# Three weight loads moved ahead of five stores in one DMA queue, and a 64-row tile that multiplies its high and low halves together

## The chip, the core and the metric

The kernel runs on one core of a Trainium2 chip, as one program. Its time is device time in microseconds (us), from launch to end; the median of three runs is what counts. One more execution was profiled, and every row below is from that one. TensorE (PE) does the matmuls, VectorE (DVE), ScalarE (ACT) and GpSimd (POOL) work on tiles, SyncE (SP) does nothing but start DMAs, in order.

## What is computed

Three layers follow each other: an attention with 32 memory slots, a dense MLP, and a mixture of eight experts with two experts per token. The change touches only the experts, which cut down read:

```
def _moe2_ref(x, w_gate, w_noise, noise, w1, w2):      # x: 2304 tokens x 512
    ...                                                # noisy logits, top 2 of 8 experts, their softmax
    for e in range(E):
        for k in range(2):
            mask = top2[:, k] == e
            h = np.maximum(x[mask] @ w1[e], 0.0)       # 512 -> 1024
            out[mask] += top2_w[mask, k, None] * (h @ w2[e])   # 1024 -> 512
```

## The kernel before

**Arithmetic.** Every float32 operand of a matmul is split into a high part (rounded to the format that TensorE takes, `F32R`) and a low part, the rest. A product is the sum of three: high x high, high x low and low x high. The splits are done by ScalarE (the high part) and VectorE (the subtraction).

**Parts.** The routing packs the tokens of each expert into a table. `PARTS` lists nine pieces of work, called parts 0 to 8 here (the index `k` in the code): parts 0 and 1 are the two pieces of expert 0, parts 2 to 8 are the other seven experts, the busiest first, and have room for 640, 640, 608, 608, 608, 576 and 576 tokens (`COLS`). Each of parts 2 to 8 has five token tiles, four of 128 rows and a last one of 128, 96 or 64 rows; the 64-row tiles are those of parts 7 and 8.

**One part.** `up(k, f)` computes the hidden units f * 128 to f * 128 + 127 of all tokens, in two column groups (of 320, 304 or 288 tokens) of 12 matmuls each, in PSUM tiles named `h` (two buffers) and `x2` (four buffers, shown as `x`) in turn. ScalarE takes the high part out of PSUM (`GH`, L675), VectorE the low part (`GL`, L676). After the eight `up` steps, `down(k, j)` multiplies token tile j with `w2`: for each f the three matmuls `GH` x hi, `GH` x lo, `GL` x hi, with the token tile held in the array and 512 columns of `w2` moving, 24 matmuls in all. VectorE scales the result by the routing weight and adds what the tokens hold already (`y`, L699), and GpSimd scatters it to `out` (L702).

**What is brought in beside that.** `fetch_w2` (L571) loads the part's own `w2` in four pieces of 512 KB on SP's queue into the tiles `w2s`, and `split_w2` splits each into high and low part (ScalarE L583, VectorE L584), between the PSUM evacuations of `up`. `gather(k + 1)` brings the next part's tokens: five indirect DMAs on GpSimd into `ex` (L621), five stores on SP's queue that put them into a scratch tensor `xs_d` (L623), and four loads that read them back in another layout as `xg` (L628). `earlier(k)` gathers the present values of `out` (L637). `fetch_w1(e + 1, c)` loads the next part's `w1` into two buffers `w1s` (L556), and `split_w1` splits it (ScalarE L568, VectorE L569). `flip` turns the gathered tokens and splits them (L654, L658, L659).

**What sets the order.** The code is written in program order, and a scheduler of the framework puts the instructions of each engine into one fixed order; `tc.issue_after(x)` tells it not to place what follows before `x`. Each engine, SP too, works through its list in order: an instruction that waits holds up everything behind it on that engine. In the loop of `experts`, the code of `gather(k + 1)` stands ahead of the four calls of `fetch_w2` (L728 to L729).

Of the kernel before, what the change touches and what calls it, by code (L numbers as in the profile page):

```python
# [6 lines left out]
F32 = mybir.dt.float32  # L7
F32R = mybir.dt.float32r
# [3 lines left out]
AF = mybir.ActivationFunctionType  # L12
OP = mybir.AluOpType
# [16 lines left out]
MAIN = 512  # L30
# [13 lines left out]
def body(ctx, tc, a):  # L44
# [10 lines left out]
    def psum(tag, bufs):  # L55
        return ps.tile([128, 512], F32, name=tag, tag=tag, bufs=bufs)
# [444 lines left out]
    LATEST = [None]  # L501
# [3 lines left out]

    m2 = ExitStack()
    P2 = {}
    W1S, W2S, W1, W2, TAB, GID, XG, EX, XH, XL, GH, GL = ({} for _ in range(12))
    PARTS = [(0, 0, EARLY), (0, EARLY, CT - EARLY)] + [(e, 0, CT) for e in range(1, E)]
    WIDTH = (EARLY * 128, CAP - EARLY * 128) + COLS  # L510
    ID, START, OVER = {}, {}, {}
# [59 lines left out]
    def fetch_w2(e, c):  # L571
        W2S[e, c] = P2["b"].tile([128, 2, DM], F32, name="w2s", bufs=4)
        w = a["moe2_w2"][bass.ds(ID[e], 1)] if e else a["moe2_w2"][0:1]
        sp.dma_start(W2S[e, c], w[:, c * 256:(c + 1) * 256, :].rearrange("o (c p) f -> p (o c) f", p=128))

    def split_w2(e, c):
        if c == 0:
# [25 lines left out]
        pool.tensor_scalar(GID[k][:, :n - 1], TAB[k][:, :n - 1, 0], float(N - 1), None, op0=OP.min)  # L603
        return pool.tensor_scalar(GID[k][:h, n - 1:], TAB[k][:h, n - 1:, 0], float(N - 1), None, op0=OP.min)

    def gather(k):
        if k < 3:
            for j in range(PARTS[k][2]):
                if k == 0:
                    XG[k, j] = m1.tile([128, DM], F32, name="xa", tag="st", bufs=4)  # L610
                elif j == 0:
                    t = P2["b"].tile([128, 4 * CT, 128], F32, name="xg").rearrange("p b c -> p (b c)")
                if k:
                    XG[k, j] = t[:, j * DM:(j + 1) * DM]
                last = pool.indirect_dma_start(out=XG[k, j], out_offset=None, in_=x2_d if k else x2_d[:KNOWN, :],
                                               in_offset=bass.IndirectOffsetOnAxis(ap=GID[k][:, j:j + 1], axis=0))
            return last
        for j in range(PARTS[k][2]):
            h = height(k, j)
            t = P2["b"].tile([128, DM], F32, name="ex", bufs=CT)[:h]  # L620
            last = pool.indirect_dma_start(out=t, out_offset=None, in_=x2_d,  # L621
                                           in_offset=bass.IndirectOffsetOnAxis(ap=GID[k][:h, j:j + 1], axis=0))
            sp.dma_start(xs_d[k % 2][j * 128:j * 128 + h, :], t)  # L623
        XG[k] = P2["b"].tile([128, 4 * CT, 128], F32, name="xg")
        w = WIDTH[k] // 32
        x = xs_d[k % 2].rearrange("(b i) (q c) -> q i b c", i=32, q=4)
        for q in range(4):
            sp.dma_start(XG[k][q * 32:(q + 1) * 32, :w, :], x[q][:, :w, :])  # L628
        return last
# [32 lines left out]
    def up(k, f):  # L662
        hi, lo = W1[PARTS[k][0]]
        c = slice(f * 128, f * 128 + 128)
        GH[k, f], GL[k, f] = [P2["b"].tile([128, CAP], F32R, name=f"g{x}{f}") for x in "hl"]
        cs = cuts(k)
        for i, (r0, r1) in enumerate(zip(cs, cs[1:])):
            r, w = slice(r0, r1), r1 - r0
            p = psum("x2", 4) if (f * (len(cs) - 1) + i) % 2 else psum("h", 2)
            n = 0  # L670
            for d in range(4):
                for wt, x in ((hi, XH[k]), (hi, XL[k]), (lo, XH[k])):
                    pe.matmul(p[:, :w], wt[:, d, c], x[:, d, r], start=(n == 0), stop=(n == 11))  # L673
                    n += 1
            act.activation(GH[k, f][:, r], p[:, :w], AF.Relu)  # L675
            LATEST[0] = dve.scalar_tensor_tensor(GL[k, f][:, r], p[:, :w], 0.0, GH[k, f][:, r].bitcast(F32),  # L676
                                                 op0=OP.max, op1=OP.subtract)

    def down(k, j, inside={}):
        e = PARTS[k][0]  # L680
        P = height(k, j)
        p = psum("x2", 4)[:P]
        hi, lo = W2[e]
        r = slice(j * 128, j * 128 + P)
        n, mm = 0, None
        for f in range(8):
            for g, w in ((GH[k, f], hi), (GH[k, f], lo), (GL[k, f], hi)):
                with tc.issue_after(mm.ins) if mm else ExitStack():
                    mm = pe.matmul(p, g[:, r], w[:, f, :], start=(n == 0), stop=(n == 23))  # L689
                n += 1  # L690
                if n in inside:
                    with tc.issue_after(mm.ins):
                        mm = inside[n]()
                elif not inside:
                    mm = None
        y = P2["b"].tile([128, DM], F32, name="y", bufs=3)[:P]
        w = TAB[k][:P, j, 1:2].bitcast(F32)
        if e:
            done = dve.scalar_tensor_tensor(y, p, w, EX[k, j], op0=OP.mult, op1=OP.add)  # L699
        else:  # L700
            done = dve.tensor_scalar(y, p, w, None, op0=OP.mult)
        st = pool.indirect_dma_start(out=a["out"], out_offset=bass.IndirectOffsetOnAxis(ap=TAB[k][:P, j, 0:1], axis=0),  # L702
                                     in_=y, in_offset=None, bounds_check=N - 1, oob_is_err=False)
        for o in puts:
            tc.declare_no_dep(st.ins, o.ins, reason="distinct rows, or ordered by the row that is read back")
        puts.append(st)
        return done

    def experts(late, last):
        open_b()  # L710
        for k, (e, t0, n) in enumerate(PARTS):
            first, nxt = t0 == 0, k + 1 < len(PARTS)
            new = nxt and PARTS[k + 1][0] != e
            if k == 1:
                gather(2)
                indices(3)
            elif k and nxt:
                with tc.issue_after(puts[-1].ins):
                    g = gather(k + 1)
                with tc.issue_after(g.ins):  # L720
                    g = earlier(k)
                if k + 2 < len(PARTS):
                    with tc.issue_after(g.ins):
                        indices(k + 2)
            elif k:
                earlier(k)
            if first:
                for c in range(4):  # L728
                    fetch_w2(e, c)  # L729
            for f in range(8):  # L730
                up(k, f)
                if k == 0 and f == 2:
                    late(15, 17)
                if k == 0 and f == 4:
                    routed = last(17, 18)
                    split_w2(e, 0)
                    split_w2(e, 1)
                    table(1)
                    with tc.issue_after(gather(1).ins):
                        table(2)  # L740
                        for c in range(2):
                            W1S[1, c] = P2["b"].tile([128, FE], F32, name="w1s", bufs=2)
                            pool.memset(W1S[1, c][:, :1], 0.0)
                            fetch_w1(1, c)
                        for i in range(3, len(PARTS)):
                            table(i)
                if first and f % 2 and (k or f > 3):
                    split_w2(e, f // 2)
            if nxt:
                flips = iter(range(PARTS[k + 1][2]))  # L750
                ahead = PARTS[k + 1][2] - n
                for j in range(max(1, (ahead + 2) // 2) if k else 0):
                    with tc.issue_after(LATEST[0].ins):
                        flip(k + 1, next(flips))
            if new and k > 1:
                for c in range(2):
                    fetch_w1(e + 1, c)
            for j in range(n):
                done = down(k, j, {} if k or j < n - 1 else {10: lambda: flip(1, 0), 18: lambda: flip(1, 1)})
                if nxt and k:  # L760
                    for i in range(max(1, (ahead + 2) // 2)):
                        i = next(flips, None)
                        if i is not None:
                            with tc.issue_after(done.ins) if k > 1 else ExitStack():
                                flip(k + 1, i)
                if new and j < 4:
                    split_w1(e + 1, j)
                    if j < 2:
                        fetch_w1(e + 1, j + 2)
            if new:  # L770
                for c in range(n, 4):
                    split_w1(e + 1, c)
                    if c < 2:
                        fetch_w1(e + 1, c + 2)
# [63 lines left out]
    first = ST.pop(("i", 0))  # L838
# [199 lines left out]
```

## Time and profile before

| | us |
|---|---|
| median of three runs | 869.5 (869.11, 869.5, 877.16) |
| the profiled execution's own time | 870.56 |
| its span, first to last instruction | 868.3 |
| outside the span | 2.26 |
| TensorE busy with matmuls | 821.9, 95% of the span |
| VectorE busy | 495.3, 57% |
| ScalarE busy | 362.4, 42% |
| GpSimd busy | 207.1, 24% |

The expert parts run from about 411 us to the end. In the profile PE is the matmuls and PEld the loading of the held operand, which overlaps them; `x<-w,gh` reads "tile x is written from tiles w and gh"; SPq is SP's DMA issues. A matmul's listed duration includes its way through the array, so for dense stretches the distance between starts is the better measure. PEclk is the TensorE clock that was granted, as a share of 2.4 GHz.

### The profile page before, as it was taken

What the parts mean: (1) busy time and instruction counts of PE and PEld (TensorE: products, weight loads), DVE (VectorE), ACT (ScalarE), POOL (GpSimd) and SP (SyncE); (2) the same over time, 40 slices, a digit from 0 to 9 for tenths busy, and PEclk for the clock granted to TensorE, in tenths of its full rate; (3) what the DMA queues carried; (4) which work ended last, traced back from release to release, by engine and by line L of the source; (5) the groups of instructions that cost most, each with busy time, mean ns of one, the idle gap of its engine ahead of it and who ended that gap; (6) DMA issues with size and microseconds to landing.
All of it is one profiled execution on the core that took longest, in us unless ns stands there. A gap on an engine that the chain in (4) does not pass through costs nothing. (4 is left out here: it accounts for less than half of the span.)

```text
span 868.3 us, 14165 instructions
## 1 busy us (share of the span) xinstructions
PE 821.9 (95%) x5276; PEld 697.9 (80%) x5276; DVE 495.3 (57%) x1161; ACT 362.4 (42%) x840; POOL 207.1 (24%) x237
## 2 busy tenths in 40 slices
PE   4598899999999999999999899999999999999994
PEld 2276667778887888887989888989889898897983
DVE  3898895875358747655724355354553546444510
ACT  3688886444434454552413343323333233332400
POOL 0243341022000500500452303215132151321301
PEclk9998999999999999999999899999999999999998
DMA  8897952274055215322463966765847657475200
GB/s 303 272 315 270 319 182 91 59 220 126 2 185 193 50 49 147 73 63 49 110 165 112 259 178 216 184 231 177 205 154 195 233 175 208 142 182 192 59 26 29
DMA packets 86254, 138.89 MB, mean 160 GB/s; under 512 B 13853, under 2 KB 48157, under 8 KB 86176
## 3 DMA queue, kind: packets, MB, share of 16 engines
q1 hardware_dynamic: 74976, 105.48, 40.8%
q0 software_dynamic: 11200, 32.43, 12.1%
q8 instruction: 43, 0.70, 0.4%
q14 instruction: 35, 0.29, 0.1%
HBM read 107.20 MB, written 31.26 MB: 159 GB/s over the span
## 5 line engine op out<-in xcount | busy, mean ns | idle before, releaser
L689 PE MATMUL x<-w,gh 128*128 128x512 f32 (+2 forms) x640 | 198.1, 390 | 0.0
L689 PEld LDWEIGHTS x<-w,gh 128*128 128x128 f32 (+2 forms) x640 | 116.6, 183 | 27.3
L689 PE MATMUL x<-w,gl 128*128 128x512 f32 (+2 forms) x320 | 124.7, 390 | 0.0
L673 PE MATMUL h<-xh,w 128*128 128x304 f32 (+4 forms) x512 | 120.4, 307 | 3.2 <-DVE gl L676 3.2
L673 PE MATMUL x<-xh,w 128*128 128x304 f32 (+4 forms) x512 | 119.0, 305 | 0.0
L280 PE MATMUL h<-ah,wph 128*128 128x320 f32 (+1 forms) x512 | 111.0, 304 | 4.8 <-DVE th L285 2.5
L280 PEld LDWEIGHTS h<-ah,wph 128*128 128x128 f32 x512 | 90.7, 193 | 20.8 <-DVE th L285 5.3
L305 PE MATMUL x<-gh,woh 128*128 128x512 f32 x256 | 105.9, 414 | 0.1
L702 POOL DMA_INDIRECT out<-y,tab x40 | 41.9, 1048 | 254.6 <-DVE y L699 221.6
L305 PE MATMUL x<-gh,wol 128*128 128x512 f32 x256 | 102.4, 400 | 0.0
L305 PE MATMUL x<-gl,woh 128*128 128x512 f32 x256 | 101.8, 398 | 0.6 <-DVE gc L299 0.3
L673 PEld LDWEIGHTS h<-xh,w 128*128 128x128 f32 x512 | 88.3, 190 | 4.1 <-DVE gl L676 3.4
L673 PEld LDWEIGHTS x<-xh,w 128*128 128x128 f32 x512 | 88.1, 190 | 0.0
L285 DVE SCALAR_TENSOR_TENSOR th<-th,h 128x256 f32<-128x256 f32 (+1 forms) x128 | 57.5, 449 | 51.9 <-ACT th L283 51.2
L489 POOL DMA_INDIRECT tab_d<-rows,slot x36 | 38.9, 1082 | 195.2 <-DVE slot L486 181.9
L283 ACT ACTIVATE th<-h 128x256 f32<-128x256 f32 (+1 forms) x128 | 52.3, 408 | 71.9 <-PE h L280 69.1
L673 PE MATMUL h<-xl,w 128*128 128x304 f32 (+4 forms) x256 | 78.4, 306 | 0.0
L673 PE MATMUL x<-xl,w 128*128 128x304 f32 (+4 forms) x256 | 78.3, 306 | 0.0
L280 PE MATMUL h<-ah,wpl 128*128 128x256 f32 (+1 forms) x256 | 76.8, 301 | 0.0
L289 ACT ACTIVATE gh<-th 128x256 fp32r<-128x256 f32 x128 | 53.3, 416 | 55.6 <-DVE th L285 55.5
L290 DVE TENSOR_TENSOR gl<-th,gh 128x256 fp32r<-128x256 f32 x120 | 54.6, 455 | 32.9 <-ACT gh L289 29.1
L699 DVE SCALAR_TENSOR_TENSOR y<-x,tab,ex 128x512 f32<-128x512 f32 (+2 forms) x35 | 26.2, 750 | 78.9 <-PE x L689 78.7
(183 smaller groups left out, 1332.3 us busy)
## 6 DMA issues: line engine op xcount, KB each, us to landing
w2s<-moe_w SPq DMA_DIRECT2D x32, 512.0 KB, 7.5
wi<-win_d SPq DMA_DIRECT2D x24, 512.0 KB, 7.1
w1s<-moe_w SPq DMA_DIRECT2D x24, 512.0 KB, 8.5
kv<-kv SPq DMA_DIRECT2D x16, 650.0 KB, 8.9
st<-moe_w_in SPq DMA_DIRECT2D x16, 512.0 KB, 5.2
st<-moe_w_out SPq DMA_DIRECT2D x16, 512.0 KB, 5.9
xs_d<-ex SPq DMA_DIRECT2D x25, 256.0 KB, 3.5
q<-qt SPq DMA_DIRECT2D x16, 288.0 KB, 5.4
```

The lines of the kernel that those rows point to most:

```text
L280: pe.matmul(p[:, :w], wt[:, g, c:c + 128], AH[b, g][at][:, t0:t0 + w], start=(n == 0), stop=(n == 5))
L283: act.activation(th[:, :w], p[:, :w], AF.Tanh, scale=0.5)
L285: dve.scalar_tensor_tensor(u[:, :w], th[:, :w], 1.0, p[:, :w], op0=OP.add, op1=OP.mult)
L289: act.activation(gh, u[:, :256], AF.Copy)
L290: last = (pool if b == 0 and (2 * f + i) % 4 == 0 else dve).tensor_sub(gl, u[:, :256], gh.bitcast(F32))
L305: pe.matmul(X2[key], held, moved, start=(f == 0 and n == 0), stop=(f == NF - 1 and n == 2))
L489: st = pool.indirect_dma_start(out=tab_d, out_offset=bass.IndirectOffsetOnAxis(ap=slot[:, j, k:k + 1], axis=0), in_=rows.bitcast(I32)[:, j ...
L673: pe.matmul(p[:, :w], wt[:, d, c], x[:, d, r], start=(n == 0), stop=(n == 11))
L689: mm = pe.matmul(p, g[:, r], w[:, f, :], start=(n == 0), stop=(n == 23))
L699: done = dve.scalar_tensor_tensor(y, p, w, EX[k, j], op0=OP.mult, op1=OP.add)
L702: st = pool.indirect_dma_start(out=a["out"], out_offset=bass.IndirectOffsetOnAxis(ap=TAB[k][:P, j, 0:1], axis=0), in_=y, in_offset=None, b ...
```

## The change

Three things change. First, the four `fetch_w2` calls stand ahead of `gather` in the code, and the stores of `gather` are told not to be placed before the last of these loads. Second, where a part has room for 576 tokens (parts 7 and 8), the second column group of `up` is taken out of PSUM in two pieces: the tokens up to 511 as before, and the last 64 into a tile `GB` of 128 columns that holds their high part in columns 0 to 63 and their low part in columns 64 to 127. `down` of the 64-row tile holds `GB` in the array and needs two matmuls per f, with hi and with lo; rows 0 to 63 of the result are the high part's share and rows 64 to 127 the low part's, and VectorE adds them in two operations. (The product low x low, which was left out before, comes in with this.) Third, the last part starts its `down` steps with the 64-row tile.

```diff
     def fetch_w2(e, c):
...
-        sp.dma_start(W2S[e, c], w[:, c * 256:(c + 1) * 256, :].rearrange("o (c p) f -> p (o c) f", p=128))
+        return sp.dma_start(W2S[e, c], w[:, c * 256:(c + 1) * 256, :].rearrange("o (c p) f -> p (o c) f", p=128))
...
-    def gather(k):
+    def gather(k, after=None):
...
-            sp.dma_start(xs_d[k % 2][j * 128:j * 128 + h, :], t)
+            with tc.issue_after(after.ins):
+                sp.dma_start(xs_d[k % 2][j * 128:j * 128 + h, :], t)
...
-            act.activation(GH[k, f][:, r], p[:, :w], AF.Relu)
-            LATEST[0] = dve.scalar_tensor_tensor(GL[k, f][:, r], p[:, :w], 0.0, GH[k, f][:, r].bitcast(F32),
-                                                 op0=OP.max, op1=OP.subtract)
+            parts = [(p[:, :w], GH[k, f][:, r], GL[k, f][:, r])]
+            if r1 == MAIN + 64:
+
+                GB[k, f] = P2["b"].tile([128, 128], F32R, name=f"gb{f}")
+                parts = [(p[:, :MAIN - r0], GH[k, f][:, r0:MAIN], GL[k, f][:, r0:MAIN]),
+                         (p[:, MAIN - r0:w], GB[k, f][:, :64], GB[k, f][:, 64:])]
+            for p, h, l in parts:
+                act.activation(h, p, AF.Relu)
+                LATEST[0] = dve.scalar_tensor_tensor(l, p, 0.0, h.bitcast(F32), op0=OP.max, op1=OP.subtract)
...
     def down(k, j, inside={}):
...
-        p = psum("x2", 4)[:P]
+        both = P == 64
+        p = psum("x2", 4)[:128 if both else P]
...
         for f in range(8):
-            for g, w in ((GH[k, f], hi), (GH[k, f], lo), (GL[k, f], hi)):
+            h, l, b = GH[k, f][:, r], GL[k, f][:, r], GB.get((k, f))
+            for g, w in ((b, hi), (b, lo)) if both else ((h, hi), (h, lo), (l, hi)):
                 with tc.issue_after(mm.ins) if mm else ExitStack():
-                    mm = pe.matmul(p, g[:, r], w[:, f, :], start=(n == 0), stop=(n == 23))
+                    mm = pe.matmul(p, g, w[:, f, :], start=(n == 0), stop=(n == (15 if both else 23)))
...
-            done = dve.scalar_tensor_tensor(y, p, w, EX[k, j], op0=OP.mult, op1=OP.add)
+            done = dve.scalar_tensor_tensor(y, p[:P], w, EX[k, j], op0=OP.mult, op1=OP.add)
+            if both:
+                done = dve.scalar_tensor_tensor(y, p[P:], w, y, op0=OP.mult, op1=OP.add)
...
+            if first:
+                for c in range(4):
+                    loaded = fetch_w2(e, c)
...
-                    g = gather(k + 1)
+                    g = gather(k + 1, loaded)
...
-            if first:
-                for c in range(4):
-                    fetch_w2(e, c)
...
-            for j in range(n):
+
+            for j in range(n) if nxt else (n - 1, *range(n - 1)):
```

**SP's queue in part 2.** These are SP's rows in the order before: `w2s` is part 2's own `w2`, `xs_d_67` the scratch tensor for part 3's tokens, `xg` their way back, `w1s` the next part's `w1`.

```order
L574 DMA w2s<-moe_w 128x2x512
L623 DMA xs_d_67<-ex 128x512 x5
L574 ISA
L574 DMA w2s<-moe_w 128x2x512
L574 ISA
L574 DMA w2s<-moe_w 128x2x512
L628 DMA xg<-xs_d_67 32x20x128 x4
L574 ISA
L574 DMA w2s<-moe_w 128x2x512
L556 ISA
L556 DMA w1s<-moe_w 128x1024
```

The same place of SP in the changed order, from the third of the four `w2s` loads on:

```order
L574 DMA w2s<-moe_w 128x2x512
L574 ISA
L574 DMA w2s<-moe_w 128x2x512
L624 DMA xs_d_67<-ex 128x512 x5
L556 ISA
L556 DMA w1s<-moe_w 128x1024
L556 ISA
L556 DMA w1s<-moe_w 128x1024
L629 DMA xg<-xs_d_67 32x20x128 x4
```

All four `w2s` loads stand ahead of the five stores now; what stands between the stores and the read-back are two `w1s` loads of the next part. In parts 3 to 8 SP's order was and stays: `w2s` loads, `w1s` loads, stores, read-back.

**ScalarE at the end of `up` in part 2.** Before, with `gh_5847` the high part of f = 7, the rows are:

```order
L675 ACTIVATE gh_5847<-h 128x320
L675 ACTIVATE gh_5847<-x_5864 128x320
L658 ACTIVATE xh<-xt 128x4x128
L583 ACTIVATE w_5673<-w2s 128x512 x2
L568 ACTIVATE w_5927<-w1s 128x512 x4
```

And in the changed order:

```order
L683 ACTIVATE gh_5847<-h 128x320
L568 ACTIVATE w_5927<-w1s 128x512
L683 ACTIVATE gh_5847<-x_5864 128x320
L568 ACTIVATE w_5927<-w1s 128x512 x3
L659 ACTIVATE xh<-xt 128x4x128 x2
```

The last two splits of `w2s` have moved up into the middle of `up`, and a split of the next part's `w1s` now stands ahead of the last evacuation of `up`; VectorE's list has the same shift.

**TensorE in part 8.** The last tile before began with these rows, with `gh_8657` and `gl_8658` for f = 0, three matmuls for each f:

```order
L689 MATMUL x_9051<-w_8721,gh_8657 64x512
L689 MATMUL x_9051<-w_8722,gh_8657 64x512
L689 MATMUL x_9051<-w_8721,gl_8658 64x512
L689 MATMUL x_9051<-w_8721,gh_8689 64x512
L689 MATMUL x_9051<-w_8722,gh_8689 64x512
```

In the changed order the tile comes first, right behind `up`'s last matmul (L674), with two matmuls for each f, and four tiles of 128 rows follow:

```order
L674 MATMUL x_8950<-xh,w_8510 128x288
L698 MATMUL x_8972<-w_8744,gb_8704 128x512
L698 MATMUL x_8972<-w_8745,gb_8704 128x512
L698 MATMUL x_8972<-w_8744,gb_8739 128x512
L698 MATMUL x_8972<-w_8745,gb_8739 128x512
```

The row count of the whole list falls from 4306 to 4290, that is 8 matmuls less for each of parts 7 and 8.

## Rows read from the trace of the kernel before

**Rows 1.** Windows: start:end length, busy PE PEld DVE ACT POOL; PEclk, DMA share, GB/s.

```profile
489.80:493.13 3.33, 0.16 (x2) 0.00 (x0) 1.14 (x3) 1.81 (x4) 1.69 (x4) 0.87 1.03 346
493.13:499.13 6.00, 6.00 (x23) 6.00 (x23) 3.44 (x7) 2.15 (x6) 0.00 (x0) 0.51 1.14 206
...
506.46:857.19 350.73, 350.73 (x1994) 312.50 (x1992) 166.43 (x289) 109.96 (x225) 93.34 (x97) 1.00 0.56 167
857.19:868.30 11.11, 0.00 (x1) 0.00 (x0) 0.74 (x1) 0.00 (x0) 0.92 (x1) 0.67 0.03 8
```

**Rows 2.** Timeline of PE in part 2: start, duration, line, tiles [idle before].

```profile
489.65 0.31 PE L673 MATMUL x<-xh,w 128*128 128x320 f32 x1
493.13 0.64 PE L673 MATMUL h<-xh,w 128*128 128x320 f32 x1 [3.17 <-DVE gl L676]
...
499.42 0.31 PE L673 MATMUL h<-xh,w 128*128 128x320 f32 x1
...
506.46 0.63 PE L689 MATMUL x<-w,gh 128*128 128x512 f32 x2
```

**Rows 3.** Timelines of ACT (two rows) and DVE (one row) in part 2.

```profile
480.37 0.65 ACT L583 ACTIVATE w<-w2s 128x512 fp32r<-128x512 f32 x1
...
491.32 0.63 ACT L583 ACTIVATE w<-w2s 128x512 fp32r<-128x512 f32 x1 [7.93 <-DMA w2s<-moe_w]
...
492.59 0.48 DVE L676 SCALAR_TENSOR_TENSOR gl<-h,gh 128x320 fp32r<-128x320 f32 x1
```

**Rows 4.** Timeline of SP's DMA issues in part 2; xN merges N issues.

```profile
466.60 0.40 SPq L574 DMA_DIRECT2D w2s<-moe_w  x1
478.37 7.66 SPq L623 DMA_DIRECT2D xs_d<-ex  x5
486.23 0.98 SPq L574 DMA_DIRECT2D w2s<-moe_w  x2
```

**Rows 5.** Timeline of POOL: the first of five gathers for part 3.

```profile
474.23 1.50 POOL L621 DMA_INDIRECT ex<-x_d,gid  x1 [0.30 <-issue]
```

**Rows 6.** Tile w2s over the whole run, its 32 loads.

```profile
DMA to landing us min/median/max: 5.1/7.5/12.9
```

**Rows 7.** Tile w1s from 470 us on, its 24 loads.

```profile
DMA to landing us min/median/max: 3.6/8.5/9.3
```

**Rows 8.** Windows, columns as in Rows 1, just ahead of the gathers.

```profile
472.00:474.00 2.00, 2.00 (x15) 1.89 (x15) 2.00 (x4) 1.64 (x3) 1.19 (x1) 1.00 0.00 0
```

**Rows 9.** Timeline of PE in part 7: its fourth and fifth tile, then part 8.

```profile
793.27 0.62 PE L689 MATMUL x<-w,gh 128*128 128x512 f32 x2
...
798.71 0.63 PE L689 MATMUL x<-w,gh 128*64 128x512 f32 x2
...
804.23 0.29 PE L673 MATMUL h<-xh,w 128*128 128x288 f32 x1
```

**Rows 10.** Groups by form, PEld of L689: count | busy, mean ns | idle before.

```profile
L689 PEld LDWEIGHTS x<-w,gh 128*128 128x128 f32 x560 | 104.5, 188 | 21.1
...
L689 PEld LDWEIGHTS x<-w,gh 128*64 128x64 f32 x32 | 4.3, 134 | 2.9
```

**Rows 11.** Groups by form: 64-column pieces on DVE and ACT, columns as in Rows 10.

```profile
L299 DVE TENSOR_TENSOR gc<-th,gc 128x64 fp32r<-128x64 f32 x64 | 17.9, 280 | 0.0
L298 ACT ACTIVATE gc<-th 128x64 fp32r<-128x64 f32 x64 | 15.6, 243 | 0.0
```

**Rows 12.** Timeline of DVE around the 64-row tile of part 7.

```profile
800.49 0.43 DVE L659 TENSOR_TENSOR xl<-xt,xh 128x256 fp32r<-128x256 f32 x1 [0.48 <-ACT xh L658]
804.43 0.74 DVE L699 SCALAR_TENSOR_TENSOR y<-x,tab,ex 64x512 f32<-64x512 f32 x1 [3.51 <-PE x L689]
```

**Rows 13.** Windows, columns as in Rows 1: a full tile's store, then the last one.

```profile
853.00:854.00 1.00, 1.00 (x6) 0.56 (x5) 0.00 (x0) 0.00 (x0) 0.70 (x1) 1.00 0.00 0
854.00:855.00 1.00, 1.00 (x6) 0.58 (x5) 0.00 (x0) 0.00 (x0) 0.00 (x0) 1.00 0.74 262
...
859.00:860.00 1.00, 0.00 (x0) 0.00 (x0) 0.00 (x0) 0.00 (x0) 0.17 (x1) 1.00 0.25 59
```

More of the change, by code (lines that the diff above doesn't have):

```diff
@@ L507, in body @@
     P2 = {}
-    W1S, W2S, W1, W2, TAB, GID, XG, EX, XH, XL, GH, GL = ({} for _ in range(12))
+    W1S, W2S, W1, W2, TAB, GID, XG, EX, XH, XL, GH, GL, GB = ({} for _ in range(13))
     PARTS = [(0, 0, EARLY), (0, EARLY, CT - EARLY)] + [(e, 0, CT) for e in range(1, E)]
```

## The prediction

> **What bounds the kernel now.** I read the busy shares first, then PE by stages, then what ended PE's idle time, and from there the queues. TensorE is busy for 95% of the span, so only two things can shorten the expert parts: fewer matmuls, or time in which PE stands still or runs slowly. The windows show where that is [rows 1]: from 506.46 us to PE's end at 857.19 its busy time equals the length of the stretch, with the clock at 1.00; there is nothing to win there but matmuls. The one hole is in part 2, at 489.80 to 493.13, and behind it a stretch at half clock (0.51, the lower level of 1.2 GHz), which ends at about 499.1.
>
> What caused it is read backwards. PE waited for VectorE's low part `gl` [rows 2], which ran at 492.59 [rows 3]. That in turn stood in VectorE's and ScalarE's lists behind a split of `w2s`, and ScalarE had waited 7.93 us for that load [rows 3]. The load was issued at 486.23 only, directly behind five stores that kept SP from 478.37 to 486.03 [rows 4]. The stores wait for GpSimd's gathers, of which the first was issued at 474.23 [rows 5]. The first `w2s` piece, which stood ahead of the stores, went out at 466.60 and was in time. So the second piece was late because of its place in SP's list, not for want of bandwidth.
>
> **The loads in front.** Cost of the hole, start to start: 493.13 - 489.65 = 3.48 us, less one matmul's distance. That distance at full clock: from 499.42 to 506.46 PE did four groups of 12, so 7.04 / 48 = 0.147 us [rows 2]. Hole: 3.33 us. From 493.13 to 506.46 it did six groups, 72 matmuls, which need 10.56 us at 0.147 and took 13.33: 2.77 us for the half clock. Together **6.10 us**. Behind it PE is dense to its end [rows 1], so what is won here is carried through.
>
> Does it all go? With the new order the second to fourth `w2s` pieces follow the first, at about 467 to 468.1 (0.49 each, from the two in 0.98 [rows 4]). The slowest `w2s` load of the run took 12.9 us [rows 6], so 481.0 is the latest landing; the median 7.5 gives 475.6. In the new order the second piece's split stands two evacuations earlier than before, directly behind the split that ran at 480.37 [rows 3], so it is wanted from about 480.9, the others some 2 us and 3.5 us later. Even the slowest would be just in time, and there is room behind it: ScalarE's wait began at 491.32 - 7.93 = 483.39 and PE stopped 6.4 us later, at 489.80; it went on 1.8 us after the wait's end. So PE would stop for a piece that lands later than 480.9 + 6.4 - 1.8 = 485.5 only. In the new order up to three splits, 1.95 us of ScalarE at most [rows 3], come between two evacuations that PE brings 1.76 us apart (12 x 0.147); the few tenths are taken up by the two buffers of `h`.
>
> What is moved past: the stores, and behind them two `w1s` loads of part 3's expert and the read-back. The stores need the gathers, which the moved 1.5 MB could slow. The DMA engines stood empty from 472 to 474 (share 0.00 [rows 8]), with the first gather at 474.23; the moved loads fill that gap and overlap the gathers until about 476 to 478, so they could hold the stores up by 3 us at most. The Trainium skill ("DMA: Bandwidth & Descriptors", Queues, rings and completion order) says that each DMA engine takes turns, packet by packet, between the queues that have work, which speaks against the move: loads put ahead take half of the gathers' engines while they last. By that rule the first store would come later and the time would stay as it is; no row of this trace shows the overlap.
>
> The new late thing can only be `w1s`. Its first two loads leave at 486.23, in the place that the `w2s` loads had, and take 8.5 us, at most 9.3 [rows 7]: landed at 494.7 to 495.5. ScalarE wants the first one behind the evacuation of `up`'s last `h` group: `up` ends at 506.46 - 6.10 = 500.36, that group 1.76 us earlier at 498.6, its evacuation by 499.0. Slack 3.5 us, or 0.5 with the stores 3 us late. And a `w1s` that is late costs nothing on PE until PE needs f = 7 of the first `down` tile, its 22nd matmul, 21 x 0.227 = 4.8 us behind 500.36. I put this at nothing; its other end is a rival below.
>
> **The pair.** A 128-row tile takes 798.71 - 793.27 = 5.44 us for 24 matmuls, 0.227 each; the 64-row tile takes 804.23 - 798.71 = 5.52, though it holds half the columns [rows 9]: the price is the moving 512 columns. Sixteen matmuls with 128 held columns, the form of the row of 5.44, take 3.63. Won: 1.89 in part 7 and 1.89 in part 8, **3.78 us**. The lower bound is what it would be if wider weight loads were in the open. A 128-column load shows 188 ns and a 64-column one 134 [rows 10], 54 ns more; 16 x 0.054 = 0.86 us a tile, leaving 0.95 each. I take the row of 5.44, since it has the same loads in it and 188 ns is under the distance of 227. The Trainium skill ("TensorE: Matmul & The Clock Gate", LDWEIGHTS) has a load's time go with the held columns, not the rows, which is the rule against this edit: the 54 ns between the rows agree with it. By that rule in the open the two tiles would save 1.9 us in all; the distances say it is hidden.
>
> Added beside PE: in each of 16 column groups one more evacuation of 64 columns, at most 0.243 us on ScalarE and 0.280 on VectorE [rows 11], in groups that PE needs some 1.6 us for (288 of 320 columns of 1.76), on engines busy 42% and 57%; the PSUM tile is held that much longer, with four buffers. Hidden. One more `y` operation for each of the two tiles, as long as the 0.74 of the first [rows 12]: in part 7 it delays the store and the gathers of `out` behind it by that, which part 8 first uses some 25 us later; in part 8 the tile is first, so it isn't at the end. The shorter tile of part 7 lets part 8 start at 802.34 instead of 804.23; its last tokens are split at 800.92 [rows 12], 1.4 us ahead. If that were late, it would cost what it is late by.
>
> **The order of the last part.** The last store is a full tile now. A full tile's bytes moved up to 855.0 at most, 1.3 us behind the end of its issue at 853.70; the last one's were done by 860.0, 0.8 behind its issue's end at 859.17 [rows 13]. So the tail of 11.11 us [rows 1] grows by about **0.5 us**. A gain is excluded, since there are no fewer rows in any store; bounds 0 (the landing is covered by what else ends the program) and 1.0 (a whole slice of the window).
>
> **Sum.** 6.10 + 3.78 - 0.5 = 9.4 us. The profiled execution had 868.3 + 2.26 = 870.56 us, so 861.2 on its scale. It stands 1.06 above the median of 869.5. If profiling costs that throughout, the median goes to 860.1; if the other runs have a smaller hole, to 861.2. No row tells; the hole can't be much smaller in them, since the half clock alone makes 2.77 of it and the fastest run is only 1.45 below. I forecast **860.3 us**, 1.06% under 869.5.
>
> **Rivals.**
>
> *The `w1s` loads inherit the stall.* They sit behind the same stores, and ScalarE has a split of them ahead of `up`'s last evacuation. For: nothing but a row of SP's list changed. Against: 3.5 us of slack, and another 6 before PE feels it. It decides from a landing at 503.9 on (505.1 less the split and the evacuation). At 507 it costs 3.1 and about 2.8 for the clock that then falls, and the time is 866.2. It ends **slower than before** from a landing at 510.5, 24 us behind the issue, where a hole of 6.6 and 2.8 of half clock have eaten the 9.4; at 513 the time is 872. That is more than twice the slowest 9.3.
>
> *Part of the hole stays,* because the moved loads share the engines with what else is there at 467 to 478 and a piece lands at 487.5 instead of 485.5. Against: that is 19 us behind its issue, and the first one, issued there, was in time. Price: 2 us of hole and a clock that stays up or falls, 862.3 to 865.1.
>
> *The pair doesn't pay:* the wider loads come out, or the 64-row tile's new waits stall PE. 862.2 to 864.1. Against: rows 9.
>
> *The change doesn't do what it says,* the hole being made elsewhere and only shown there. 3.3 us from the pair alone, 866.2. Against: the chain from the store to the hole has no link without a row.
>
> **How the numbers follow.** The forecast gets 0.76, the pair that doesn't pay 0.08, the inherited stall with a gain left 0.05 and slower than before 0.03, a hole that stays in part 0.05, the last 0.03. The forecast's own spread: upward 0.5 for the tail's bound and up to 1.45 for a smaller hole, downward 0.5 for the tail and 0.4, by which the fastest run lies under the median; so 859.4 to 862.3. The range of 858.6 to 863.6 takes in the nearer parts of the rivals. About 1% is what a measurement of this kernel can tell from no change: 860.8. It lies within the forecast's spread, with some 0.7 of it below: 0.53 faster, and the rest with the rivals that keep a gain or none, 0.44; 0.03 slower.
>
> **What would show it.** Right: SP's four `w2s` issues together at 466 to 468 us; no wait of ScalarE for `w2s` in part 2; PE dense from 472 to its end with the clock at 1.00; `up` of part 2 ending at about 500.4; the tiles of 64 rows at 3.6 us each; PE's end at about 847.3; a tail of 11.6. Wrong: a wait of PE at about 505, a distance above 0.227 in the 64-row tiles, or idle time ahead of part 8's first matmul.

## The result, and the profile after

The changed kernel takes **862.69 us** (median of five runs, 860.93 to 865.03). The kernel before, run beside it, took 872.91 us (869.11 to 877.16). The ratio of the runs is 0.9891, with a 95% interval of 0.9861 to 0.9920 (that of the two medians is 0.9883): **1.1% faster**. The forecast was 860.3 with a range of 858.6 to 863.6, 1.06% under the 869.5 known then.

I compare the two traces by one stretch, from the first `up` matmul of part 2 to the end of TensorE's last matmul. It holds all of the change but the tail, and what happens ahead of part 2 can't blur it. Before it took 857.19 - 471.85 = 385.34 us. After it takes 850.85 - 475.39 = 375.46. The difference is **9.88 us; the two terms of the sum gave 6.10 + 3.78 = 9.88.** (That it agrees to the hundredth owes something to luck: both terms were read from this same profile of before, and against its second profile, further down, the difference is 7.66.)

First SP's DMA issues in part 2 of the kernel after (start, duration, line, tiles), against [rows 4]:

```profile
470.10 2.62 SPq L574 DMA_DIRECT2D w2s<-moe_w  x4
482.09 8.34 SPq L624 DMA_DIRECT2D xs_d<-ex  x5
490.69 0.96 SPq L556 DMA_DIRECT2D w1s<-moe_w  x2
492.79 3.24 SPq L629 DMA_DIRECT2D xg<-xs_d  x4
```

All four `w2s` loads leave together, 5.29 us ahead of the stretch (before, the first did so 5.25 us ahead). The first store follows the first gather (477.76) by 4.33 us, where it was 4.14 in [rows 4, 5]. Next ScalarE's splits in the same part, against [rows 3]; a bracket would be idle time and what ended it:

```profile
483.07 0.64 ACT L583 ACTIVATE w<-w2s 128x512 fp32r<-128x512 f32 x1
483.90 1.69 ACT L583 ACTIVATE w<-w2s 128x512 fp32r<-128x512 f32 x3
485.78 1.18 ACT L583 ACTIVATE w<-w2s 128x512 fp32r<-128x512 f32 x2
487.14 1.19 ACT L583 ACTIVATE w<-w2s 128x512 fp32r<-128x512 f32 x2
...
503.95 0.63 ACT L568 ACTIVATE w<-w1s 128x512 fp32r<-128x512 f32 x1 [1.17 <-PE x L674]
```

The wait of 7.93 us is gone, and the first `w1s` split, where the stall might have gone, waits for a matmul and not for a load. What PE makes of it, by windows (start:end length, busy time of PE, PEld, DVE, ACT, POOL; granted clock, DMA share, GB/s), against [rows 1]:

```profile
475.39:503.89 28.50, 28.50 (x195) 28.25 (x194) 14.72 (x28) 11.74 (x26) 12.17 (x13) 1.00 0.91 258
503.89:850.85 346.96, 346.95 (x1978) 312.12 (x1976) 168.46 (x305) 111.16 (x239) 92.98 (x97) 1.00 0.57 169
850.85:861.80 10.95, 0.00 (x0) 0.00 (x0) 0.75 (x1) 0.00 (x0) 0.97 (x1) 0.69 0.08 28
```

`up` of part 2 takes 28.50 us with PE full throughout, and PE stays full at clock 1.00 to its end. The tail of 11.11 has become 10.95. The 64-row tile of part 7 and the first matmul of part 8, in PE's timeline, against [rows 9]:

```profile
796.15 3.80 PE L698 MATMUL x<-w,gb 128*128 128x512 f32 x16
799.78 0.29 PE L674 MATMUL h<-xh,w 128*128 128x288 f32 x1
```

From start to start it is 3.63 us, where it was 5.52: won 1.89 in part 7.

The stretch began 3.54 us later than before, though up to part 2's `w2s` loads every engine's list is the same. The two profiled executions differ, piece by piece, as follows: 870.56 - 9.88 (stretch) + 3.54 (ahead of it) - 0.16 (tail) - 0.50 (outside the span: 1.76, before 2.26) = 863.56. The 0.50 comes with the programs: the time outside the span is 2.12 to 2.27 us in all runs of before that have it, 1.73 to 1.80 in those of after, and no run shows why. The 3.54 is a balance. Until 353 us after was 2.62 us ahead of before, most of it won from 68 to 77 us, where the granted clock was 0.62 in before and 1.00 in after. Two holes then cost it some 6 us, with the half clock behind the first; "issue" means that the profile shows nothing that PE waited for:

```profile
356.49 0.62 PE L280 MATMUL h<-ah,wph 128*128 128x256 f32 x2 [2.59 <-issue]
...
457.45 0.28 PE L674 MATMUL h<-xl,w 128*128 128x256 f32 x1 [1.02 <-issue]
```

### The profile page after: what moved, and what is told of

Its sections match the earlier page's. It is cut to its first block, busy times and chain, and to the rows that moved or that the text cites. A ratio compares the mean times of both kernels' runs of the same rounds, so it can differ in the third digit from the quotient of the medians.

```text
span 861.8 us, 14168 instructions
## 1 busy us (share of the span) xinstructions
PE 813.7 (94%) x5260; PEld 693.9 (81%) x5260; DVE 497.9 (58%) x1179; ACT 364.1 (42%) x856; POOL 206.9 (24%) x237
## 4 chain that ended last, share of the span: by engine, by line
PE 80%; DVE 8%; ACT 4%; DMA 3%; issue 2%; POOL 1%; SPq 1%; POOLq 0%; ACTq 0%
PE x L698 25%; PE x L305 18%; PE x L674 12%; PE h L674 12%; PE h L280 9%; PE aux L149 2%; DMA st<-moe_w_out 1%; DMA kv<-kv 1%; DVE gl L290 1%; PE aux L127 1%; DVE th L285 1%; POOL wo L224 1%; ACT lw L203 1%; DVE wo L209 1%; ACT th L283 1%
## 5 line engine op out<-in xcount | busy, mean ns | idle before, releaser
L698 PE MATMUL x<-w,gh 128*128 128x512 f32 (+1 forms) x608 | 188.0, 390 | 0.0
L698 PEld LDWEIGHTS x<-w,gh 128*128 128x128 f32 (+1 forms) x608 | 112.4, 186 | 24.4
L674 PE MATMUL h<-xh,w 128*128 128x304 f32 (+4 forms) x512 | 119.1, 304 | 0.3 <-issue 0.3
L698 PE MATMUL x<-w,gl 128*128 128x512 f32 (+1 forms) x304 | 118.5, 390 | 0.0
L674 PE MATMUL x<-xh,w 128*128 128x304 f32 (+4 forms) x512 | 118.0, 303 | 0.0
L674 PEld LDWEIGHTS h<-xh,w 128*128 128x128 f32 x512 | 87.4, 188 | 2.1 <-issue 1.5
L674 PEld LDWEIGHTS x<-xh,w 128*128 128x128 f32 x512 | 87.2, 188 | 0.0
L674 PE MATMUL h<-xl,w 128*128 128x304 f32 (+4 forms) x256 | 77.8, 304 | 1.0 <-issue 1.0
L674 PE MATMUL x<-xl,w 128*128 128x304 f32 (+4 forms) x256 | 77.8, 304 | 0.0
```

The source lines that it names most:

```text
L698: mm = pe.matmul(p, g, w[:, f, :], start=(n == 0), stop=(n == (15 if both else 23)))
```

## Experiments

My theory: two independent gains, a stall that the order of SP's list put into ScalarE's list, and eight matmuls fewer in each of two tiles. The rivals: all of the gain is the pair's and the stall only moves; or the reverse; or the loads are late in themselves, wherever they stand. The first four kernels ran on one chip, where the kernel before took 871.12 us (median of 22 runs).

**The loads alone.** Edit, on the kernel before (with `return` in `fetch_w2`):

```diff
-    def gather(k):
+    def gather(k, after=None):
...
-            sp.dma_start(xs_d[k % 2][j * 128:j * 128 + h, :], t)
+            with tc.issue_after(after.ins):
+                sp.dma_start(xs_d[k % 2][j * 128:j * 128 + h, :], t)
...
+            if first:
+                for c in range(4):
+                    loaded = fetch_w2(e, c)
             if k == 1:
...
-                    g = gather(k + 1)
+                    g = gather(k + 1, loaded)
...
-            if first:
-                for c in range(4):
-                    fetch_w2(e, c)
```

> The kernel before with the first edit alone: the four w2 loads ahead of the stores, no pair tile, no new order of the last part. Measure: from the first up matmul of part 2 to the end of TensorE's work, 385.34 us in the profile of before and 375.46 in that of after. My theory (the loads of w2 stood behind stores that waited for gathers, so a split of w2 waited in ScalarE's queue in front of the evacuations) takes away the hole of 3.33 us and the half clock of 2.77 us behind it and nothing else: stretch 379.2 us, ScalarE without a wait for w2s in part 2, granted clock 1.00 from there to the end of TensorE's work, tail 11.1 us as before; total about 6 us under before, ratio about 0.993. Rival (the gain of after came from the pair tiles, and the wait only moved to another load): the stretch stays at 383 to 385 us, with a hole that ends at a w1s or xg load.

Measured: 865.80 us, ratio 0.9935 (0.9918 to 0.9953). The stretch, in one window of its trace:

```profile
474.14:853.39 379.25, 379.25 (x2187) 340.75 (x2185) 179.63 (x315) 120.51 (x249) 105.25 (x110) 1.00 0.59 174
```

It is 379.25 us, against 379.2 expected; PE is full, the clock 1.00, and ScalarE has no wait for `w2s` (a bracket would show it):

```profile
482.65 1.69 ACT L583 ACTIVATE w<-w2s 128x512 fp32r<-128x512 f32 x3
...
485.89 1.19 ACT L583 ACTIVATE w<-w2s 128x512 fp32r<-128x512 f32 x2
```

The tail is 864.3 - 853.39 = 10.9. So the reorder alone takes away hole and half clock, and the rival that moves the stall falls.

**The pair alone.** Edit: all of the diff in `up` and `down`; `fetch_w2`, `gather` and the order of the last part stay as they were before.

```diff
+            if r1 == MAIN + 64:
+                GB[k, f] = P2["b"].tile([128, 128], F32R, name=f"gb{f}")
...
-            for g, w in ((GH[k, f], hi), (GH[k, f], lo), (GL[k, f], hi)):
+            h, l, b = GH[k, f][:, r], GL[k, f][:, r], GB.get((k, f))
+            for g, w in ((b, hi), (b, lo)) if both else ((h, hi), (h, lo), (l, hi)):
```

> The kernel before with the second edit alone: pair tiles in the last two parts, the loads where they were, the tiles of the last part in their old order. My theory: the hole of about 3.3 us and the half clock stay in part 2, each tile of 64 rows takes 3.6 us and not 5.52, so the stretch from the first up matmul of part 2 to TensorE's end is 385.34 - 3.78 = 381.6 us; total about 3.8 us under before, ratio about 0.9957. Rival (the pair's added evacuations and weight loads eat its gain): stretch 383.5 to 385.5 us, with TensorE waiting in the up matmuls of the last two parts. The last tile has 64 rows and two vector operations behind its last matmul: tail 11.1 to 11.6 us.

Measured: 868.00 us, ratio 0.9962 (0.9946 to 0.9979); the stretch is 854.42 - 472.87 = 381.55 us, against 381.6. The stall is there, in ScalarE's and PE's timelines, and the windows show the clock behind it:

```profile
493.60 0.63 ACT L583 ACTIVATE w<-w2s 128x512 fp32r<-128x512 f32 x1 [9.18 <-DMA w2s<-moe_w]
```

```profile
495.41 0.63 PE L673 MATMUL h<-xh,w 128*128 128x320 f32 x1 [4.43 <-DVE gl L683]
...
850.63 3.79 PE L697 MATMUL x<-w,gb 128*128 128x512 f32 x16
```

```profile
495.41:497.00 1.59, 1.59 (x6) 1.59 (x7) 0.54 (x1) 0.00 (x0) 0.00 (x0) 0.50 1.18 219
497.00:498.00 1.00, 1.00 (x6) 1.00 (x5) 0.07 (x1) 0.74 (x2) 0.00 (x0) 0.50 1.00 197
498.00:499.00 1.00, 1.00 (x7) 1.00 (x7) 1.00 (x2) 1.00 (x4) 0.00 (x0) 0.76 1.11 230
```

The two edits add up: 0.9935 x 0.9962 = 0.9897, beside 0.9891 for both. The parts of the stall differ, though: over the 375.46 of after this stretch has 6.09 us, of which 4.43 are idle time and 1.66 the half clock. Before, counted by the same bracket (3.17, [rows 2]), the half clock's share is 385.34 - 379.25 - 3.17 = 2.92. The sum agreed and its parts did not. The tail, 866.2 - 854.42 = 11.8, is over the 11.1 to 11.6 expected; the next run shows what was priced too low.

**The short tile last.** Edit, on the kernel after:

```diff
-            for j in range(n) if nxt else (n - 1, *range(n - 1)):
+            for j in range(n):
```

> After with the last part's tiles in their old order, so that the 64-row tile comes last with its two vector operations. My prediction charged 0.5 us to the tail for a last tile of 128 rows; the profile of after shows 10.95 us from TensorE's end to the end of the span, against 11.11 before. If the bytes of the last store set the tail, this kernel's is 10.5 to 10.8 us; if the number of operations behind the last matmul does, it is 11.2 to 11.4 (one more vector operation of 0.28 us); if neither, 10.9 to 11.2. The stretch from the first up matmul of part 2 to TensorE's end stays at 375.5 us in all three. Total within 0.5 us of after.

Measured: 861.22 us (861.04 to 861.82), ratio 0.9889 (0.9872 to 0.9906); the stretch is 847.78 - 472.33 = 375.45 us, the tail 859.4 - 847.78 = **11.6**, a little more than any of the three expectations. Its last two vector operations:

```profile
847.82 0.74 DVE L708 SCALAR_TENSOR_TENSOR y<-x,tab,ex 64x512 f32<-64x512 f32 x1 [2.88 <-PE x L698]
848.60 0.75 DVE L710 SCALAR_TENSOR_TENSOR y<-x,tab,y 64x512 f32<-64x512 f32 x1
```

The second one sets the store back by 0.78, not by the 0.28 that I had put in from narrower pieces. The bytes hardly show. From the end of the last store's issue to the end of the span it is 859.4 - 850.55 = 8.85 us with 64 rows here, and 861.8 - 852.88 = 8.92 with 128 rows in the kernel after; over all the profiles it is 8.85 to 9.28, in no order of rows. The bytes do land later: in the second profiles of before and after, further down, the last store lands 2.6 us behind its issue with 64 rows and 3.3 with 128. What ends the program covers most of that. In whole runs the two orders can't be told apart: after had 860.93 to 865.03.

**The splits put back.** The kernel before, SP's list untouched, with the late splits of part 2 taken out of the way of the evacuations (`EVAC[0]` is the last of them):

```diff
-            act.activation(GH[k, f][:, r], p[:, :w], AF.Relu)
+            EVAC[0] = act.activation(GH[k, f][:, r], p[:, :w], AF.Relu)
...
-                if first and f % 2 and (k or f > 3):
+                if first and f % 2 and (k or f > 3) and (k != 2 or f < 2):
                     split_w2(e, f // 2)
+            if k == 2:
+                for c in range(1, 4):
+                    with tc.issue_after(EVAC[0].ins):
+                        split_w2(e, c)
```

> The kernel before, with SyncE's order untouched (three of the four w2 loads of part 2 still behind the stores), and the second to fourth split of w2 in part 2 put behind the last evacuation of up in ScalarE's queue. It asks what the hole is made of. My theory (a late load costs only because its split stands in front of evacuations in an in-order queue): no hole near 490, up ends about 28.5 us after its start; then the splits have their data (landed by 491 to 494, the fourth load by about 502) and feed the down matmuls with a hole of at most 1 us, or up to 4 if the fourth load or the split's rate is late: stretch 379.2 to 383 us, most likely 379.6. Rival (the weights of part 2 are late in themselves, whoever waits): the same 3 us or more are missed at the first down matmuls, with the half clock behind: stretch 384 to 386 us.

Measured: 868.01 us, ratio 0.9968 (0.9950 to 0.9987); the stretch is 855.34 - 473.26 = 382.08 us, between the likeliest 379.6 and the rival's 384. ScalarE's timeline, then PE's:

```profile
502.30 2.18 ACT L583 ACTIVATE w<-w2s 128x512 fp32r<-128x512 f32 x4
507.84 1.15 ACT L583 ACTIVATE w<-w2s 128x512 fp32r<-128x512 f32 x2 [3.36 <-DMA w2s<-moe_w]
```

```profile
501.76 0.62 PE L689 MATMUL x<-w,gh 128*128 128x512 f32 x2
...
508.52 1.22 PE L689 MATMUL x<-w,gh 128*128 128x512 f32 x3 [2.04 <-ACT w L583]
```

There is no hole near 490, and `up` takes 501.76 - 473.26 = 28.50 us, as in after: the second and third load, issued at 489.14 behind the stores, cost nothing, since no evacuation stood behind their splits. That is the theory. But the fourth load, issued at 494.88 behind the read-back, was wanted at about 504.5, and its split started at 507.84: a hole of 2.04 us that the theory had only as its upper end. (The other 0.79 over 379.25 lies in the same `down`, in no hole that the timeline lists.) The order of ScalarE's list made the hole of before; a second, smaller one lay behind it, which among these runs only the earlier loads removed.

**A longer wait.** The kernel before, with the second to fourth load behind the read-back too, and the second split held ahead of the evacuations from the fourth column block on:

```diff
-                    fetch_w2(e, c)
+                    with tc.issue_after(BACK[0].ins) if k == 2 and c else ExitStack():
+                        fetch_w2(e, c)
...
+                if k == 2 and f == 3:
+                    split_w2(e, 1)
...
+            with tc.issue_after(SPLIT[0].ins) if k == 2 and f >= 3 else ExitStack():
+                act.activation(GH[k, f][:, r], p[:, :w], AF.Relu)
```

> The dose: the kernel before, with the second to fourth w2 load of part 2 not only behind the stores but behind the four xg loads too, and the second split of w2 held in ScalarE's queue where it stood, ahead of the evacuations from the fourth column block on. In the loads-only run xg's issues end about 5 us later than the two w2 issues of before, and a w2 load issued behind them landed 10 to 13 us after its issue (the fourth load of the run with the splits put back). My theory: the hole in the up matmuls starts where it started, about 18 us after the first up matmul, and ends with the later load: 9 to 14 us in place of 3.3, the half clock behind it once, so the stretch from the first up matmul of part 2 to TensorE's end is 385.3 + 6 to 11 = 391 to 396 us, total about 1% over before. Rival (what ends the hole is not this load but the DMA engines being full at that time, or the half clock): the stretch stays within 2 us of 385.3.

This run and the two below were on another chip, where the kernel before took 865.90 us. Measured: 877.90, ratio 1.0137 (1.0098 to 1.0176); the stretch is 867.21 - 471.53 = 395.68 us, inside 391 to 396.

```profile
504.26 1.15 ACT L585 ACTIVATE w<-w2s 128x512 fp32r<-128x512 f32 x2 [21.18 <-DMA w2s<-moe_w]
```

```profile
506.67 0.63 PE L677 MATMUL h<-xh,w 128*128 128x320 f32 x1 [13.51 <-DVE gl L681]
```

```profile
506.67:508.00 1.33, 1.33 (x5) 1.33 (x6) 1.33 (x4) 1.33 (x5) 0.00 (x0) 0.50 0.57 228
...
513.00:514.00 1.00, 1.00 (x9) 1.00 (x8) 0.39 (x1) 0.44 (x1) 0.00 (x0) 1.00 0.00 0
```

The load is later, the hole is longer, and it ends with that load: 13.51 us. It began later than I said, 21.6 us into the stretch, since the matmuls were laid in another order. Over 379.25 the stretch has 16.43 us, so the half clock behind the hole took 2.92, as in before.

**Before and after, once more.** The two kernels without an edit, for the holes ahead of part 2.

> The kernel before, unchanged, profiled a second time. Every profile of a changed kernel has one or two holes of 0.4 to 2.6 us ahead of part 2, at 354 to 358 us and at 453 to 457 us, most of them with no wait that the profile shows; the profile of before has none over 0.7 us there. If these holes come and go by themselves, this profile has some too, and the stretch from the first up matmul of part 2 to TensorE's end is again 384.5 to 386.5 us. If the changed programs cause them, there are none here again.

> After, unchanged, profiled a second time, for the same question: if the holes ahead of part 2 come and go, the first up matmul of part 2 comes earlier here than at 475.4 us (between 471.5 and 474.5), and the stretch from it to TensorE's end is again 375.4 to 375.6 us, since TensorE has no hole in it. If they belong to this program, part 2 starts at 475 again. Tail 10.8 to 11.1.

Measured: before 865.95 us, after 857.50, one run each. Neither has a hole of 0.7 us or more between 170 and 465 us; part 2 starts at 469.81 and at 469.15, for after earlier than I had said. The stretch of after is again 844.61 - 469.15 = 375.46, with a tail of 11.1. The stretch of before is 852.93 - 469.81 = 383.12, **below** the expected 384.5:

```profile
490.93 0.42 PE L673 MATMUL h<-xh,w 128*128 128x320 f32 x1 [3.01 <-DVE gl L676]
495.02 0.42 PE L673 MATMUL h<-xh,w 128*128 128x320 f32 x1 [0.30 <-DVE gl L676]
```

```profile
490.93:493.00 2.07, 2.07 (x14) 2.07 (x15) 0.68 (x2) 0.80 (x2) 0.00 (x0) 1.00 1.10 222
493.00:494.00 1.00, 1.00 (x9) 1.00 (x8) 1.00 (x2) 1.00 (x4) 0.00 (x0) 1.00 1.21 261
```

The first hole is the same and the clock did not fall; the two holes are 3.31, and 0.57 is spread over the rest. So there the loads in front save 383.12 - 375.46 - 3.78 = 3.88 us and not 6.10, with the pair taken at its 3.78. The question about the holes is answered in part: this chip shows none in before, in after or in the longer wait. The first chip shows them in all four kernels. Before has none in either of its profiles and after has them in one of two, so the program of after doesn't always make them; whether the chip does is not settled.

## Why the prediction was right

**The loads in front** (6.10 us) held: 385.34 - 379.25 = 6.09 in the run with that edit alone. The links of the chain that was read backwards held. The two runs on the wait show it from both sides: take the splits from in front of the evacuations and the hole near 490 goes with SP's list unchanged; delay the load and the hole grows with it. What the chain did not show was the second late load, 2.04 us with the splits put back; reordering ScalarE's list instead would have left it.

**Size of that term.** The 2.77 us of half clock (2.92 by the bracket) is the part that doesn't come every time: 2.92, 1.66 and 2.92 us behind holes of 3.17, 4.43 and 13.51 us, and none behind one of 3.01. The prediction said that the hole "can't be much smaller" in other runs because the half clock alone made 2.77 of it. That step was wrong, and in the second pair of profiles the same reorder is worth 2.2 us less.

**What the loads were moved past.** The prediction gave the stores up to 3 us of delay. The two profiles on the second chip both have landing times; there the summary of DMA issues from 464 to 512 us (name, queue, count, median us to landing) reads in before

```profile
xs_d<-ex SPq DMA_DIRECT2D x5, 256.0 KB, 3.4
...
ex<-x_d,gid POOLq DMA_INDIRECT x5, 4.8
```

and in after

```profile
xs_d<-ex SPq DMA_DIRECT2D x5, 256.0 KB, 5.2
...
ex<-x_d,gid POOLq DMA_INDIRECT x5, 6.8
```

The gathers did slow, by 2 us, and the stores' issues ended 13.2 us after the start of the first gather and not 11.3 (12.7 and 11.8 in the first pair of profiles). The rule that the prediction weighed (the Trainium skill, "DMA: Bandwidth & Descriptors", Queues, rings and completion order: queues with work take turns on a DMA engine) fits these rows, though they don't show the turns themselves; it decided nothing of the time. The read-back landed at about 502.5 (12.0 us behind its last issue). Its first reader, `flip` on VectorE, started at 504.00 right behind other work, with no wait for it, and part 3's `up` some 22 us later than the landing. The `w1s` rival had no row for it in any of the runs with the loads in front: the first split waits for a matmul.

**The pair** (3.78 us) held: 379.25 - 375.45 = 3.80 between the run with the loads alone and the one with both and the old order. The new evacuations took 223 ns on ScalarE and 224 on VectorE, under the 243 and 280 of the bound. The wider weight loads stayed hidden: the groups of weight loads by form show the pair's 32 at 188 ns, as the other 128-column ones, under the distance of 227. By the rule weighed there (the Trainium skill, "TensorE: Matmul & The Clock Gate", LDWEIGHTS: a load's time goes with its held columns) the load is dearer, and the rows agree (188 ns, against 134 for 64 columns [rows 10]); it is not in the open, and the two tiles save twice the 1.9 us that it would have left.

```profile
L698 PEld LDWEIGHTS x<-w,gb 128*128 128x128 f32 x32 | 6.0, 188 | 1.2
```

**The order of the last part** is the term that was mis-sized, though small: +0.5 us was charged for the bytes of a full last tile, and the tail became 0.16 shorter (about 0.2 longer in the second pair of profiles). The full tile's bytes do land later, 3.3 us behind the issue against 2.6, but what ends the program, some 9 us behind that issue, covers most of it: the sum's bound of 0 and not its 0.5. That "a gain is excluded" was too strong, since the time behind the last issue moves by 0.4 us from profile to profile. Against the natural choice for the pair, the short tile last, this order saves 0.5 to 0.7 us of tail, about one vector operation of 0.75.

**The time.** The median came out 2.4 us over 860.3, inside the range, with the kernel before 3.4 over the 869.5 that the forecast was measured from. The profile's own account puts the miss ahead of the stretch, where I had assumed the two kernels to be alike: without those 3.54 us the profiled pair would lie 10.5 apart, and the medians lie 10.2 apart. That the median fell inside the range in absolute terms is in part luck, since the kernel before moved by as much as the miss.

## What to carry to other kernels

A late load can cost more through what stands behind its consumer in an in-order list than through the consumer itself: follow the wait to the list it blocks, and then to what the load itself stood behind. Where an engine is full from one point to the end, one window from there repeats to 0.01 us (375.46, 375.45 and 375.46 in three profiles), while whole runs of one kernel spread by up to 8; with a hole in it, it doesn't (385.34 and 383.12 for the kernel before). Half-clock time behind a hole should be priced as a range from nothing up, not as part of the hole.

## What was not expected of the hardware

The granted clock does not follow the length of a hole alone. After a hole of 3.01 us it stayed at 1.00; after one of 3.17 in the same program it was 0.51 over the next 6.00 us [rows 1]. In the kernel after, a hole of 2.59 in an earlier stage lowered it, and one of 1.02 did not; the 2.04 with the splits put back did not either:

```profile
356.49:360.00 3.51, 3.51 (x12) 3.02 (x13) 2.51 (x6) 2.59 (x7) 0.00 (x0) 0.53 0.00 0
```

What else decides it, no run here shows.

Holes of 0.2 to 2.6 us came up near 354 to 359 and 453 to 457 us in five profiles, the first of after and the four on the first chip, and in none of the other four. Most of them nothing in the profile ends ("issue"); in some PE waited for an engine that itself waited for PE. The DMA engines were busy a few microseconds earlier, but so they were where there was no hole: from 350 to 352 us their share was 0.82 in after and 0.96 in before. Late instruction fetches do not explain the earlier place: in none of the five profiles is a packet of an instruction queue listed from 348 to 360 us. The cause stays open.
